# Start-up and x loads of a fused short convolution and ELU layer: band read in place, x of super 1 queued behind w_in, batch zeros over loaded rows, idle matmuls in super 0

## The chip, the cores and the metric

The kernel runs on one core of a Trainium2 chip. The time is the device time of one execution in microseconds. Executions of one kernel mostly agree within 0.3% of their median. Every ratio below is taken on one chip and within one set of rounds. The granted clock is the share of its full speed at which TensorE was allowed to run, by the profiler's records; "half clock" is a share of 0.5.

## The reference

`x` is (8, 4096, 192). A causal depthwise convolution of 7 taps is applied along the sequence, with one softmax-normalised set of taps for each of 8 heads of 24 channels. Then comes a two-layer network with ELU, 192 to 2048 to 192, over all 32768 tokens.

```python
w = softmax(weight)                       # (8 heads, 7 taps)
x_pad = concatenate([zeros(B, 6, D), x])  # zeros before each batch
out[b, s] = sum_k w[head, k] * x_pad[b, s + k]
h = out.reshape(32768, 192) @ w_in        # 192 -> 2048
g = where(h > 0, h, exp(min(h, 0)) - 1)
result = g @ w_out                        # 2048 -> 192
```

## The kernel before

The tokens are cut into 32 super-tiles ("supers") of 1024 tokens; four make a batch. Each super goes through 16 chunks of 128 hidden features. For each chunk TensorE makes H, ScalarE makes exp(H) into E, POOL clamps E to at most 1, and VectorE makes max(E - 1, H) as gT; one super later TensorE multiplies gT by w_out. H has three slots, so TensorE can be at most three chunks (or convs) ahead of VectorE. Two half convs per super are made by TensorE as well, with windows of x as weights and a band matrix `Tm` as the moving operand. Their result is evacuated to `csb`, written to HBM (`conv_slots`) and read back in another layout (`att`).

The band is built at the start: zeros are written to HBM, the 7 taps are written over the diagonal by a strided DMA, and all is read back as `Tk`, with the heads innermost. ScalarE and VectorE then each copy half of it to `Tm`, where the columns of one head lie together:

```python
# SyncE
sy.dma_start(diagonal, wprb[:].rearrange("p k h -> p (k h)")).then_inc(s_band, 16)
W(s_band, 32)
sy.dma_start(Tk[:], band[:, :, :]).then_inc(s_band, 16)
# ScalarE; VectorE does the other four heads in the same way
W(s_band, 48)
a.activation(Tm[:, HEADS // 2 :, :].rearrange("p h t -> p t h"),
             Tk[:, :, HEADS // 2 :], ACT.Copy).then_inc(s_tm)
# TensorE, in the conv
pe.matmul(H[...], xg[:, s % NXB, w, CPH * h : CPH * (h + 1)],
          Tm[:, h, PAD + c0 : PAD + c0 + nc_], ...)
```

POOL issues the loads of x and w_in, which convert from fp32 to bf16:

```python
X_AT = ((2, 0), (4, 1), (12, 2))       # (chunk, part of x of super s + 2)
# [cut]
def load_x(s, part):
    # [cut] part 0 exists only where a batch starts
    if part == 0:
        g.memset(xg[0:PAD, b, 0, :], 0.0).then_inc(s_z)
        g.dma_start(xg[PAD:P, b, 0, :], x_flat[t0 : t0 + P - PAD, :]).then_inc(s_x[b][0], 16)
        return
    # [cut] part 1: windows 0 (or 1) to 4; part 2: windows 5 to 8
for part in range(3):
    load_x(0, part)
W(s_band, 32)                          # the diagonal has landed
load_w_in(0)
W(s_w[0], 48)
g.dma_start(w_in[HP:P, :, c0:c1], w_in[0:HP, :, c0:c1]).then_inc(s_wdp, 16)
W(s_cv, 2)                             # both convs of super 0 are done
for part in range(3):
    load_x(1, part)
```

TensorE also runs 34 matmuls on zeros at the start and 24 after the first convs (`warm`), to keep its clock up.

Of the kernel before, what the change touches and what calls it, by code (L numbers as in the profile page):

```python
# [12 lines left out]
P = 128  # L13
# [3 lines left out]
HEADS = 8  # L17
# [4 lines left out]
CW = 122  # L22
# [6 lines left out]
NG3 = 2  # L29
LAG = -1  # L30
QA = 8
WARM = (34, 24)
HALF_STEPS = (10, 10, 6, 6, 10, 11, 11)

CONV_AT = ((4, 1, 1), (12, 2, 0))
EARLY_CONV = {1: (1, 0), 4: (1, 1), 12: (2, 0)}
XW = 5
X_AT = ((2, 0), (4, 1), (12, 2))
W_OUT_AT = 8

PIECES = (
# [6 lines left out]
def bass_lightweight_conv__then__act_elu_kernel(  # L48
# [84 lines left out]
    with ExitStack() as stack:  # L133
# [73 lines left out]
        NDMA_ATT = 6  # L207
        x_need, z_need, x_count, z_count = {}, {}, [0] * NXB, 0
        for s in range(NS):
            x_count[s % NXB] += 16 + 16 * (s % SPB == 0)  # L210
            z_count += s % SPB == 0
            x_need[s, 0] = x_count[s % NXB]
            x_need[s, 1] = 16 * (s // NXB + 1)
            z_need[s] = z_count
# [30 lines left out]
        @block.gpsimd  # L245
        def _gpsimd(g: bass.BassGpSimd):
            W = Waits(g)

            def load_x(s, part):
                b, t0 = s % NXB, s * SUP  # L250
                first = s % SPB == 0
                if part == 0 and not first:
                    return
                if s >= NXB:
                    W(s_cv, 2 * (s - NXB) + 2)
                if part == 0:
                    g.memset(xg[0:PAD, b, 0, :], 0.0).then_inc(s_z)
                    g.dma_start(  # L258
                        xg[PAD:P, b, 0, :], x_flat[t0 : t0 + P - PAD, :]
                    ).then_inc(s_x[b][0], 16)  # L260
                    return
                if part == 1:
                    w0, w1, row = int(first), XW, t0 - PAD + CW * first
                else:
                    w0, w1, row = XW, NWIN, t0 + SUP - P - CW * (NWIN - 1 - XW)
                src = bass.AP(
                    tensor=x_flat.tensor,
                    offset=row * D,
                    ap=[[D, P], [CW * D, w1 - w0], [1, D]],
                )  # L270
                g.dma_start(xg[:, b, w0:w1, :], src).then_inc(s_x[b][part - 1], 16)  # L271

            def load_w_in(k):
                c0, c1 = WCOLS[k]
                for j in range(3):
                    g.dma_start(  # L276
                        w_in[0:HP, j, c0:c1],
                        bass.AP(
                            tensor=moe_w_in.tensor,
                            offset=8 * j * FF + c0,  # L280
                            ap=[[CPH * FF, HEADS], [FF, 8], [1, c1 - c0]],
                        ),
                    ).then_inc(s_w[k], 16)

            for part in range(3):
                load_x(0, part)
            W(s_band, 32)
            load_w_in(0)
            W(s_w[0], 48)
            c0, c1 = WCOLS[0]  # L290
            g.dma_start(w_in[HP:P, :, c0:c1], w_in[0:HP, :, c0:c1]).then_inc(s_wdp, 16)
            W(s_cv, 2)
            for part in range(3):
                load_x(1, part)
            W(s_att[0], 16 * NDMA_ATT)
            load_w_in(1)
            for n in range(NP):
                s, i = divmod(n, NQ)
                if n == W_OUT_AT:
                    g.dma_start(  # L300
                        w_out[:, :, :], moe_w_out.rearrange("(q p) d -> p q d", p=FC)
                    ).then_inc(s_w[2], 16)
                for at, part in X_AT:
                    if at == i and s + NXB < NS:
                        load_x(s + NXB, part)
                for u in range(2):
                    W(s_exp, 2 * n + u + 1)
                    g.tensor_scalar(  # L308
                        out=E[:, n % NE, u, :],
                        in0=E[:, n % NE, u, :],  # L310
                        scalar1=1.0,
                        scalar2=0.0,
                        op0=ALU.min,
                        op1=ALU.max,
                    ).then_inc(s_clp)

        @block.scalar
        def _scalar(a):
            W = Waits(a)
            a.memzero(scr[:, 0:1]).then_inc(s_scr)  # L320
            W(s_scr, 1)
            a.activation(scr[:, 1:2], scr[:, 0:1], ACT.Exp)
            W(s_set, 2)
            a.activation(wex[:], wq2[:], ACT.Exp).then_inc(s_wex)
            W(s_band, 48)
            a.activation(  # L326
                Tm[:, HEADS // 2 :, :].rearrange("p h t -> p t h"),
                Tk[:, :, HEADS // 2 :],
                ACT.Copy,
            ).then_inc(s_tm)  # L330

            def evac(t, half):
                n_half = 2 * t + half
                W(s_mm2, n_half + 1)
                b = n_half % 2
                W(s_out[b], 32 * (n_half // 2))
                if (t, half) == last_half:
                    a.activation(  # L338
                        osb[:, b, 0, :, :].rearrange("p k d -> p (k d)"),
                        H[:, last_slot % 3, 0 : 2 * D],  # L340
                        ACT.Copy,
                    ).then_inc(s_oev)
                    W(s_od, 1)
                    out_group(a, t, half, 1)
                    return
                a.activation(  # L346
                    osb[:, b, :, :, :].rearrange("p g k d -> p g (k d)"),
                    ops[:, :, 0 : 2 * D],
                    ACT.Copy,
                ).then_inc(s_oev)  # L350

            for item in order:
                if item[0] == "c":
                    m = item[1]
                    if m == 1:
                        W(s_dw[0], 16)
                        read_att(a, W, 0, 0)
                        continue
                    W(s_cv, m + 1)
                    W(s_dw[m % 4], 16 * (m // 4))  # L360
                    a.activation(  # L361
                        csb[:, m % 4, :, :],
                        H[:, slot_of_conv[m] % 3, :].rearrange("p (b t) -> p b t", b=2),
                        ACT.Copy,
                    ).then_inc(s_ce)
                elif item[0] == "h":
                    n = item[1]
                    k = slot_of_pair[n] % 3
                    W(s_h, n + 1)
                    W(s_tt, 2 * (n - NE) + 2)  # L370
                    for u in range(2):
                        a.activation(  # L372
                            E[:, n % NE, u, :], H[:, k, GS * u : GS * (u + 1)], ACT.Exp
                        ).then_inc(s_exp)
                else:
                    _, t, half, r0, r1 = item
                    if r1 == NR:
                        evac(t, half)

        @block.vector  # L380
        def _vector(v):
# [21 lines left out]
                ALU.mult,  # L403
            ).then_inc(s_set)
            v.memset(H[:, 0:2, :], 0.0).then_inc(s_hz)
            W(s_band, 48)
            v.tensor_copy(  # L407
                Tm[:, 0 : HEADS // 2, :].rearrange("p h t -> p t h"), Tk[:, :, 0 : HEADS // 2]
            ).then_inc(s_tm)
            W(s_cv, 2)  # L410
            v.tensor_copy(
                csb[:, 1, :, :],
                H[:, slot_of_conv[1] % 3, :].rearrange("p (b t) -> p b t", b=2),
            ).then_inc(s_cd)
            for n in range(NP):
                s, q = divmod(n, NQ)
                if s >= NG3:
# [20 lines left out]
        def _tensor(pe):  # L438
# [17 lines left out]
            for item in order:  # L456
                if item[0] == "c":
                    m = item[1]
                    s, g = divmod(m, 2)
                    if m == 0:  # L460
                        W(s_tm, 2)
                        W(s_hz, 1)
                    for part in range(g + 1):
                        W(s_x[s % NXB][part], x_need[s, part])
                    W(s_z, z_need[s])
# [2 lines left out]
                    for hb in range(2):  # L468
                        for (w, c0, nc_, o) in PIECES[g]:
                            for q in range(4):  # L470
                                h = 4 * hb + q
                                ins = pe.matmul(  # L472
                                    H[SLOT * q : SLOT * q + CPH, k % 3,
                                      GS * hb + o : GS * hb + o + nc_],
                                    xg[:, s % NXB, w, CPH * h : CPH * (h + 1)],
                                    Tm[:, h, PAD + c0 : PAD + c0 + nc_],
                                    start=True,
                                    stop=True,
                                    tile_position=(0, SLOT * q),
                                )  # L480
                    ins.then_inc(s_cv)
                elif item[0] == "h":
                    n = item[1]
                    s, q = divmod(n, NQ)
                    if n == 0:
                        warm(WARM[1])
                    W(s_w[q // QA], 48)
                    W(s_wdp if q < QA else s_wd[1], 16)
                    W(s_att[s % 2], 16 * NDMA_ATT * (s // 2 + 1))
# [131 lines left out]
```

## Time and profile before

| | before |
|---|---|
| time, median (range, 3 runs) | 786.17 us (785.61 to 786.69) |
| profiled span | 783.9 us |
| first exp of chunk 0 | 29.62 us |
| from there to the first exp of super 1 | 26.69 us |
| a super after that | 22.95 us; 23.62 us for seven of them |

The last three rows come from the starts of ScalarE's exp instructions in the trace: chunk 0 of each super marks its beginning.

These are lines of the page of the kernel before: the span, TensorE's busy time, the granted clock in 40 slices (tenths), and the group of conv matmuls with their count, total busy us and mean ns.

```profile
span 783.9 us, 32275 instructions
...
PE 751.1 (96%) x13882; PEld 514.9 (66%) x13882; DVE 638.0 (81%) x1035; ACT 658.4 (84%) x1156; POOL 663.3 (85%) x1116
...
PEclk9889999999999999999999999999999999999999
...
L472 PE MATMUL H<-Tm,xg 128*24 128x122 bf16 (+1 forms) x2560 | 43.1, 213 | 7.4 <-DVE gT L421 5.0
```

TensorE is busy 96% of the span and about 98.5% of each 100 us window after the start.

The next lines are from the chain of waits of the kernel before, at the start: start in us, duration in us, what the chain stood on. "DMA" is a transfer from issue to landing.

```profile
5.50 3.22 DMA conv_band<-wprb
...
8.73 2.69 DMA Tk<-conv_band
...
11.44 2.55 ACT Tm L326
...
14.04 1.94 PE H L472 x75
...
17.25 6.92 DMA conv_slots<-csb
...
25.59 2.39 DMA att<-conv_slots
...
28.12 1.48 PE H L494 x6
```

Everything here is serial. Note the slot write at 17.25: 6.92 us, where the page's median for this transfer is 3.2 us. The packet records show what shares the DMA engines with it: 1152 packets of 384 bytes, x of super 1, between 19.3 and 24.5 us.

The third excerpt is the chain of the kernel before, inside super 6, one of the seven long ones.

```profile
175.06 0.19 POOL xg L257
175.25 0.54 POOL xg L258
...
175.82 2.34 POOL E L308 x4
178.16 0.75 POOL xg L271
...
178.94 0.64 POOL E L308
...
179.60 1.30 DVE gT L421 x2
```

POOL zeroes six rows (0.19 us of chain), issues the extra load of a batch start (0.54) and, a little later, the usual load (0.75). All of it stands between the clamps that VectorE and then TensorE wait for.

### The profile page before, as it was taken

Reading aid. Unit: us, or ns where it says so; the run is one execution under the profiler, and the core shown is the slowest. Engines: PE = TensorE matmul, PEld = TensorE weight load, DVE = VectorE, ACT = ScalarE, POOL = GpSimd, SP = SyncE. Lnnn points to the kernel's source line nnn. Section 1 sums busy time; section 2 is a strip of 40 time slices with the busy share of each in tenths; the row PEclk is TensorE's granted clock in tenths of the full one; section 3 lists DMA queues with packets and bytes.
Section 4 is the critical chain, followed back from the end, with each engine's and each line's share of the span. In section 5 each row is a group of like instructions: output and inputs, shape, how many; then the busy total and the mean of one; then the engine's idle time right before and its main releaser. Section 6 shows DMA issues by size and latency. Waiting matters only on the chain.

```text
span 783.9 us, 32275 instructions
## 1 busy us (share of the span) xinstructions
PE 751.1 (96%) x13882; PEld 514.9 (66%) x13882; DVE 638.0 (81%) x1035; ACT 658.4 (84%) x1156; POOL 663.3 (85%) x1116
## 2 busy tenths in 40 slices
PE   8479999999999999999999999999999999999997
PEld 3136666766666666666676666666667666666766
DVE  3378888888888888888888888888888888888893
ACT  2478888898889888888888888988888988898883
POOL 3488988988888898898898888889889889888882
PEclk9889999999999999999999999999999999999999
DMA  6674344344344435434444433443443444444212
GB/s 106 113 120 88 83 109 86 90 109 104 76 104 92 101 87 112 93 79 111 83 91 109 109 81 93 83 111 89 110 92 84 107 83 94 104 111 83 77 42 63
DMA packets 108031, 73.71 MB, mean 94 GB/s; under 512 B 45520, under 2 KB 106960, under 8 KB 107888
## 3 DMA queue, kind: packets, MB, share of 16 engines
q1 hardware_dynamic: 66344, 55.14, 22.2%
q0 software_dynamic: 41056, 16.11, 19.3%
q8 instruction: 109, 1.79, 0.9%
q10 hardware_dynamic: 488, 0.39, 0.2%
q14 instruction: 34, 0.28, 0.1%
HBM read 44.31 MB, written 42.24 MB: 110 GB/s over the span
## 4 chain that ended last, share of the span: by engine, by line
PE 41%; POOL 38%; DVE 11%; ACT 5%; DMA 2%; issue 2%; SPq 0%
POOL E L308 32%; PE H L494 24%; PE ops L523 16%; DVE gT L421 10%; POOL xg L271 6%; ACT E L372 5%; DMA conv_slots<-csb 1%; PE H L523 1%; POOL xg L258 0%; DMA conv_band<-wprb 0%; PE H L472 0%; DMA wq<-in_weight_dram 0%; DMA Tk<-conv_band 0%; ACT Tm L326 0%; DMA att<-conv_slots 0%
## 5 line engine op out<-in xcount | busy, mean ns | idle before, releaser
L421 DVE SCALAR_TENSOR_TENSOR gT<-E,H 128x512 f16<-128x512 f32 x1024 | 631.1, 682 | 123.1 <-POOL E L308 122.5
L308 POOL TENSOR_SCALAR E<-E 128x512 f32<-128x512 f32 x1024 | 602.0, 614 | 85.9 <-ACT E L372 77.4
L372 ACT ACTIVATE E<-H 128x512 f32<-128x512 f32 x1024 | 548.7, 597 | 97.8 <-PE H L494 81.4
L494 PE MATMUL H<-att,w_in 64*128 64x512 bf16 x3072 | 409.2, 379 | 19.6 <-DVE gT L421 10.1
L523 PE MATMUL ops<-w_out,gT 64*128 64x192 f16 x8064 | 414.7, 243 | 0.9 <-DVE gT L421 0.9
L523 PEld LDWEIGHTS ops<-w_out,gT 64*128 64x128 f16 x8064 | 342.7, 94 | 109.9 <-DVE gT L421 1.1
L494 PEld LDWEIGHTS H<-att,w_in 64*128 64x128 bf16 x3072 | 130.5, 94 | 125.0 <-DVE gT L421 30.8
L361 ACT ACTIVATE csb<-H 128x1024 bf16<-128x1024 f32 x63 | 64.5, 1023 | 5.4 <-PE H L472 5.2
L346 ACT ACTIVATE osb<-ops 128x768 f32<-128x768 f32 x63 | 51.5, 818 | 5.1 <-PE ops L523 5.1
L271 POOL DMA_DIRECT2D xg<-in_x_dram x64 | 53.1, 830 | 0.4 <-PE H L472 0.4
L472 PE MATMUL H<-Tm,xg 128*24 128x122 bf16 (+1 forms) x2560 | 43.1, 213 | 7.4 <-DVE gT L421 5.0
L472 PEld LDWEIGHTS H<-Tm,xg 128*24 128x24 bf16 x2560 | 33.5, 94 | 19.4 <-issue 16.5
L453 PE MATMUL ops<-zw 128*128 128x512 bf16 x58 | 16.5, 454 | 1.2 <-DVE zw L383 1.2
L276 POOL DMA_DIRECT2D w_in<-in_moe_w_in_dram x6 | 3.5, 584 | 15.7 <-DMA att<-conv_slots 10.3
L453 PEld LDWEIGHTS ops<-zw 128*128 128x128 bf16 x58 | 6.4, 113 | 10.6 <-issue 5.1
L326 ACT ACTIVATE Tm<-Tk 128x544 bf16<-128x544 bf16 x1 | 2.5, 2542 | 7.0 <-DMA Tk<-conv_band 7.0
L432 DVE COPY osb<-H 128x384 f32<-128x384 f32 x1 | 0.6, 558 | 8.9 <-PE H L523 8.9
L523 PE MATMUL H<-w_out,gT 64*128 64x192 f16 x128 | 5.6, 243 | 0.1
L523 PEld LDWEIGHTS H<-w_out,gT 64*128 64x128 f16 x128 | 5.2, 94 | 0.3 <-PE H L523 0.3
L258 POOL DMA_DIRECT2D xg<-in_x_dram x8 | 4.8, 602 | 0.3 <-issue 0.3
L407 DVE COPY Tm<-Tk 128x544 bf16<-128x544 bf16 x1 | 1.3, 1335 | 3.9 <-DMA Tk<-conv_band 3.9
L338 ACT ACTIVATE osb<-H 128x384 f32<-128x384 f32 x1 | 0.5, 490 | 4.7 <-PE H L523 4.7
(20 smaller groups left out, 11.3 us busy)
## 6 DMA issues: line engine op xcount, KB each, us to landing
out_dram<-osb SPq DMA_DIRECT2D x127, 192.0 KB, 2.4
conv_slots<-csb SPq DMA_DIRECT2D x64, 256.0 KB, 3.2
att<-conv_slots SPq DMA_DIRECT2D x189, 64.0 KB
xg<-in_x_dram POOLq DMA_DIRECT2D x40, 192.0 KB, 3.8
xg<-in_x_dram POOLq DMA_DIRECT2D x24, 240.0 KB, 4.5
w_in<-in_moe_w_in_dram POOLq DMA_DIRECT2D x6, 128.0 KB, 3.8
w_out<-in_moe_w_out_dram POOLq DMA_DIRECT2D x1, 768.0 KB, 8.8
w_in<-w_in POOLq DMA_DIRECT2D x1, 384.0 KB, 4.6
```

The lines of the kernel that those rows point to most:

```text
L258: g.dma_start(xg[PAD:P, b, 0, :], x_flat[t0 : t0 + P - PAD, :]).then_inc(s_x[b][0], 16)
L271: g.dma_start(xg[:, b, w0:w1, :], src).then_inc(s_x[b][part - 1], 16)
L276: g.dma_start(w_in[0:HP, j, c0:c1], bass.AP(tensor=moe_w_in.tensor, offset=8 * j * FF + c0, ap=[[CPH * FF, HEADS], [FF, 8], [1, c1 - c0]], ...
L308: g.tensor_scalar(out=E[:, n % NE, u, :], in0=E[:, n % NE, u, :], scalar1=1.0, scalar2=0.0, op0=ALU.min, op1=ALU.max,).then_inc(s_clp)
L346: a.activation(osb[:, b, :, :, :].rearrange("p g k d -> p g (k d)"), ops[:, :, 0 : 2 * D], ACT.Copy,).then_inc(s_oev)
L361: a.activation(csb[:, m % 4, :, :], H[:, slot_of_conv[m] % 3, :].rearrange("p (b t) -> p b t", b=2), ACT.Copy,).then_inc(s_ce)
L372: a.activation(E[:, n % NE, u, :], H[:, k, GS * u : GS * (u + 1)], ACT.Exp).then_inc(s_exp)
L421: v.scalar_tensor_tensor(out=gT[:, s % NG3, q, u, :], in0=E[:, n % NE, u, :], scalar=1.0, in1=H[:, slot_of_pair[n] % 3, GS * u : GS * (u + ...
L453: pe.matmul(ops[:, 0, :], zw[:, 0:P], zw[:], start=True, stop=True)
L472: ins = pe.matmul(H[SLOT * q : SLOT * q + CPH, k % 3, GS * hb + o : GS * hb + o + nc_], xg[:, s % NXB, w, CPH * h : CPH * (h + 1)], Tm[:, ...
L494: ins = pe.matmul(H[:, k % 3, GS * r : GS * (r + 1)], w_in[HP * r : HP * (r + 1), j, FC * q : FC * (q + 1)], att[HP * r : HP * (r + 1), s ...
L523: ins = pe.matmul(acc[:, g, D * kb : D * (kb + 1)], gT[HP * rt : HP * (rt + 1), t % NG3, q, g, t0 : t0 + P], w_out[HP * rt : HP * (rt + 1) ...
```

## The change

There are four parts. (1) The first conv reads `Tk` in place, so no copy stands before it; one copy on VectorE follows the csb copy. (2) POOL queues w_in at once, without waiting for the diagonal, and x of super 1 right behind it. (3) At a batch start the rows of window 0 are loaded with the others and then overwritten with zeros, which saves a DMA issue. (4) Two matmuls on zeros precede most H chunks of super 0, to keep the clock up.

```diff
-WARM = (34, 24)
+WARM = (34, 24, 2)
-X_AT = ((2, 0), (4, 1), (12, 2))
+X_AT = ((4, 1), (10, 0), (12, 2))
# POOL, load_x
-                if part == 0:
-                    g.memset(xg[0:PAD, b, 0, :], 0.0).then_inc(s_z)
-                    g.dma_start(
-                        xg[PAD:P, b, 0, :], x_flat[t0 : t0 + P - PAD, :]
-                    ).then_inc(s_x[b][0], 16)
+                if part == 0:
+                    if s:
+                        W(s_x[b][0], x_need[s, 0])
+                    g.memset(xg[0:PAD, b, 0, :], 0.0).then_inc(s_z)
+                    if s == 0:
+                        g.dma_start(
+                            xg[PAD:P, b, 0, :], x_flat[0 : P - PAD, :]
+                        ).then_inc(s_x[b][0], 16)
# POOL, start
-            W(s_band, 32)
             load_w_in(0)
+            for part in range(3):
+                load_x(1, part)
             W(s_w[0], 48)
             # [cut] the copy of w_in to the other partitions
-            W(s_cv, 2)
-            for part in range(3):
-                load_x(1, part)
# ScalarE and VectorE: the two half copies before the first conv go; VectorE, after its csb copy:
+            v.tensor_copy(Tm[:, :, :].rearrange("p h t -> p t h"), Tk[:]).then_inc(s_tm)
# TensorE, conv
-                                    Tm[:, h, PAD + c0 : PAD + c0 + nc_],
+                                    Tm[:, h, PAD + c0 : PAD + c0 + nc_]
+                                    if s
+                                    else Tk[:, PAD + c0 : PAD + c0 + nc_, h],
# TensorE, H
+                    elif n < NQ - 1:
+                        warm(WARM[2])
# [cut] semaphore counts
```

More of the change, by code (lines that the diff above doesn't have):

```diff
@@ L209, in bass_lightweight_conv__then__act_elu_kernel @@
         for s in range(NS):
-            x_count[s % NXB] += 16 + 16 * (s % SPB == 0)
+            x_count[s % NXB] += 16 + 16 * (s == 0)
             z_count += s % SPB == 0
@@ L253, in load_x @@
                     return
+                if part == 0:
[6 more added lines that the diff above has]
+                        ).then_inc(s_x[b][0], 16)
+                    return
                 if s >= NXB:
                     W(s_cv, 2 * (s - NXB) + 2)
-                if part == 0:
-                    g.memset(xg[0:PAD, b, 0, :], 0.0).then_inc(s_z)
-                    g.dma_start(
-                        xg[PAD:P, b, 0, :], x_flat[t0 : t0 + P - PAD, :]
-                    ).then_inc(s_x[b][0], 16)
-                    return
                 if part == 1:
-                    w0, w1, row = int(first), XW, t0 - PAD + CW * first
+                    w0, w1, row = int(s == 0), XW, t0 - PAD + CW * (s == 0)
                 else:
@@ L324, in _scalar @@
             a.activation(wex[:], wq2[:], ACT.Exp).then_inc(s_wex)
-            W(s_band, 48)
-            a.activation(
-                Tm[:, HEADS // 2 :, :].rearrange("p h t -> p t h"),
-                Tk[:, :, HEADS // 2 :],
-                ACT.Copy,
-            ).then_inc(s_tm)
             def evac(t, half):
@@ L405, in _vector @@
             v.memset(H[:, 0:2, :], 0.0).then_inc(s_hz)
-            W(s_band, 48)
-            v.tensor_copy(
-                Tm[:, 0 : HEADS // 2, :].rearrange("p h t -> p t h"), Tk[:, :, 0 : HEADS // 2]
-            ).then_inc(s_tm)
             W(s_cv, 2)
@@ L460, in _tensor @@
                     if m == 0:
-                        W(s_tm, 2)
+                        W(s_band, 48)
                         W(s_hz, 1)
+                    if m == 2:
+                        W(s_tm, 1)
                     for part in range(g + 1):
```

## The prediction

> **What bounds the kernel now.** From 56 us on, TensorE is busy about 98.5% of every 100 us window (the table of windows) at full clock; a super-tile (16 chunks) takes 22.95 us, so nothing here makes that rate better. But every fourth one (those loading x for a new batch; 7 in all) takes 23.62 us: 0.67 us more, and TensorE idles 0.54 us before the conv there. Before that, the chain of waits is serial: weights, band (written 5.50, 3.2 us; read back 8.73, 2.7 us), copy to Tm 11.44 (ScalarE 2.54 us), conv 14.04, its slots written from 17.25 (6.92 us to landing, against a median of 3.2 us), att read, first H matmul only at 28.12. Super 0 then takes 26.7 us, with TensorE busy 19.6 of the 28 us from 28 to 56 and half clock for 24.2 to 31.0 and 48.1 to 54.9 (clock records).
>
> **The steps.**
>
> 1. *Band in place.* The 2.55 us Tm copy leaves the chain, its replacement on VectorE (an estimated 2.7 us, twice the 1.33 us half) runs after the csb copy, off it. Price: the moving operand steps 16 bytes. The Trainium skill ("SBUF — State Buffer", Door 1: The DMA port swizzle) says every access to a new 16-byte line pays; no trace here shows it yet. The conv took 1.94 us cold; I expect about the same, warm but strided.
>
> 2. *Queue.* w_in no longer waits for the band, so it shares the DMA engines with the band's read-back; "DMA: Bandwidth & Descriptors" (Queues, rings and completion order) says engines round-robin between queues by packet. Tk has 128 packets of 93 ns, w_in 192 of some 200 ns: I expect Tk about 1.2 us later (12.6). Net conv start: 12.6 instead of 14.04, 1.4 us gained.
> In exchange, x of super 1 (1152 packets of 50 ns, 19 to 25 us in the packet records) no longer collides with the slot writes; part of the w_in copy still does. The second write should land near 19.5 instead of 24.17, the first H matmul start at 23.3 instead of 28.1: 4.8 us gained with step 1.
>
> 3. *Idle matmuls.* 28 of them, about 0.22 us warm: 6 us of TensorE time, mostly into its 8.4 us of idle time. They remove the half clock at 48 to 55 us, where the 12 H matmuls at 51.80 took 2.74 us on the chain instead of some 1.5. The first H chunk may still be cold. Small delays when two chunks are ready together. Net 1 us.
>
> 4. *Batch zeros.* Seven DMA issues (0.59 us) and their memset (0.25 us) leave chunk 2, where VectorE work is waiting for POOL; the memset reappears in chunk 10, in a stretch where POOL is also continuous. I take back 0.15 of the 0.67 us: 7 x 0.52 = 3.6 us.
>
> **Prediction: 776.8 us** (786.2 - 4.8 - 1.0 - 3.6), 8 in 10 within 772.5 to 781. Faster by over 2%: 0.05; within 2%: 0.94; slower: 0.01.
>
> **What would show it.** Step 1: first conv starts before 13 us; 80 matmuls within 2.2 us. Step 2: second slot write lands in 3 to 5 us; first H matmul at 22 to 24.5. Step 3: no half-clock stretch after 31 us; super 0 near 25.7 us. Step 4: all periods within 0.2 us of 22.95; no 0.54 us idle before the conv.
>
> **What would make it wrong.** Strided reads slowing the conv 3-fold (1.5 us lost or more); w_in traffic delaying the band read by 3 us; the w_in copy, now queued behind 1152 x packets, becoming what H waits for; idle matmuls hit at half clock (0.43 us each) delaying chunk 1; the memset in chunk 10 costing all of its 0.25 us.

## The result and the profile after

The changed kernel took 780.68 us (780.54 to 780.74, 4 runs) against 785.89 us of the kernel before on the same chip: ratio 0.9932, 95% interval 0.9915 to 0.9949. That is inside the predicted range, but the gain is 5.2 us where 9.4 us were predicted.

From the exp starts of the two traces, the 5.15 us of the spans divide as follows:

| stage | before | after | measured | predicted |
|---|---|---|---|---|
| start of the first H matmul | 28.12 | 26.80 | -1.32 | -4.8 |
| from there to the first exp | 1.50 | 0.87 | -0.63 | "may still be cold" |
| super 0, first exp to first exp of super 1 | 26.69 | 26.47 | -0.22 | -1.0 |
| supers 1 to 30 | 692.05 | 689.07 | -2.98 | -3.6 |

Lines of the page of the changed kernel that answer to those of before; the conv matmuls now stand in two groups, packed (`Tm`) and in place (`Tk`).

```profile
span 778.7 us, 32323 instructions
...
PE 755.2 (97%) x13910; PEld 515.3 (66%) x13910; DVE 639.0 (82%) x1035; ACT 655.4 (84%) x1155; POOL 660.0 (85%) x1109
...
PEclk9999999999999999999999999999999999999999
...
L466 PE MATMUL H<-Tm,xg 128*24 128x122 bf16 (+1 forms) x2480 | 41.1, 210 | 0.6 <-DVE gT L413 0.6
...
L466 PE MATMUL H<-Tk,xg 128*24 128x122 bf16 (+1 forms) x80 | 3.9, 363 | 5.4 <-DMA Tk<-conv_band 5.4
```

The in-place matmuls take 363 ns on average, the packed ones 210. The clock row no longer has the two 8s of the second and third slices.

The chain of waits of the changed kernel, over the start and most of super 0:

```profile
5.50 6.26 DMA conv_band<-wprb
...
11.78 3.67 DMA Tk<-conv_band
...
15.50 3.89 PE H L466 x74
...
20.67 2.17 DMA conv_slots<-csb
...
24.25 2.41 DMA att<-conv_slots
...
26.80 0.83 PE H L492 x6
27.63 0.67 PE ops L445 x2
...
30.66 0.88 PE ops L445 x2
...
32.29 0.54 PE ops L445 x2
...
39.25 0.54 PE ops L445 x2
```

Read against the chain of before, the copy is gone (-2.55). But the diagonal takes 6.26 instead of 3.22 (+3.04), the read-back 3.67 instead of 2.69 (+0.98), and the conv 3.89 instead of 1.94 (+1.95). Only the slot write pays for it: 2.17 instead of 6.92 (-4.75). The sum is -1.33, which is the -1.32 of the table. The idle matmuls (`PE ops L445`) stand on the chain four times, 2.63 us together.

The chain of the changed kernel inside super 9, an ordinary super, shows half of a period:

```profile
240.24 3.52 POOL E L310 x6
243.76 0.82 POOL xg L275
...
244.62 0.63 POOL E L310
...
245.27 1.30 DVE gT L413 x2
...
246.62 1.47 PE H L492 x12
```

The six clamps and the issue of a load at chunk 4 are on the chain (0.82 us; the load at chunk 12 of the same super takes another 0.73); TensorE, "busy" 99% of the time, is waiting for them through VectorE.

### The profile page after: what moved, and what is told of

Read it like the earlier page. It is cut to its first block, busy times and chain, and to the rows that moved or that the text cites. A ratio compares the mean times of both kernels' runs of the same rounds, so it can differ in the third digit from the quotient of the medians.

```text
span 778.7 us, 32323 instructions
## 1 busy us (share of the span) xinstructions
PE 755.2 (97%) x13910; PEld 515.3 (66%) x13910; DVE 639.0 (82%) x1035; ACT 655.4 (84%) x1155; POOL 660.0 (85%) x1109
## 4 chain that ended last, share of the span: by engine, by line
PE 41%; POOL 38%; DVE 11%; ACT 5%; DMA 2%; issue 2%; SPq 0%
POOL E L310 32%; PE H L492 24%; PE ops L521 15%; DVE gT L413 10%; POOL xg L275 6%; ACT E L367 5%; DMA conv_band<-wprb 1%; PE H L521 1%; PE H L466 1%; DMA Tk<-conv_band 0%; DMA wq<-in_weight_dram 0%; PE ops L445 0%; DMA att<-conv_slots 0%; DMA conv_slots<-csb 0%; POOL xg L258 0%
## 5 line engine op out<-in xcount | busy, mean ns | idle before, releaser
L275 POOL DMA_DIRECT2D xg<-in_x_dram x64 | 53.8, 842 | 0.4 <-issue 0.4
L466 PE MATMUL H<-Tm,xg 128*24 128x122 bf16 (+1 forms) x2480 | 41.1, 210 | 0.6 <-DVE gT L413 0.6
L466 PEld LDWEIGHTS H<-Tm,xg 128*24 128x24 bf16 x2480 | 31.6, 93 | 11.6 <-issue 11.6
L445 PE MATMUL ops<-zw 128*128 128x512 bf16 x86 | 23.2, 407 | 1.2 <-DVE zw L378 1.2
L445 PEld LDWEIGHTS ops<-zw 128*128 128x128 bf16 x86 | 7.4, 102 | 14.0 <-issue 7.0
L466 PE MATMUL H<-Tk,xg 128*24 128x122 bf16 (+1 forms) x80 | 3.9, 363 | 5.4 <-DMA Tk<-conv_band 5.4
L466 PEld LDWEIGHTS H<-Tk,xg 128*24 128x24 bf16 x80 | 2.2, 115 | 7.1 <-DMA Tk<-conv_band 5.9
```

The lines of the kernel that those rows point to most:

```text
L275: g.dma_start(xg[:, b, w0:w1, :], src).then_inc(s_x[b][part - 1], 16)
L445: pe.matmul(ops[:, 0, :], zw[:, 0:P], zw[:], start=True, stop=True)
L466: ins = pe.matmul(H[SLOT * q : SLOT * q + CPH, k % 3, GS * hb + o : GS * hb + o + nc_], xg[:, s % NXB, w, CPH * h : CPH * (h + 1)], Tm[:, ...
```

## The experiments

Eleven kernels were built from the changed one, and one (batch zeros alone) from the kernel before. All gave correct results.

| run | median | before, same chip | ratio (95%) |
|---|---|---|---|
| changed kernel | 780.68 | 785.89 | 0.9932 (0.9915 to 0.9949) |
| diagonal first | 780.24 | 786.89 | 0.9927 (0.9914 to 0.9940) |
| no idle matmuls | 781.99 | 786.89 | 0.9936 (0.9922 to 0.9951) |
| Tm copies back | 781.98 | 786.89 | 0.9948 (0.9933 to 0.9963) |
| all convs in place | 851.78 | 786.89 | 1.0833 (1.0817 to 1.0850) |
| batch zeros alone | 783.89 | 785.22 | 0.9974 (0.9959 to 0.9990) |
| x after the band | 782.25 | 785.22 | 0.9955 (0.9938 to 0.9973) |
| packed band | 779.63 | 785.22 | 0.9922 (0.9906 to 0.9939) |
| POOL loads at 6, 14 | 791.13 | 785.22 | 1.0066 (1.0051 to 1.0081) |
| POOL loads at 5, 13 | 769.48 | 785.96 | 0.9789 (0.9769 to 0.9808) |
| other start-up order | 780.03 | 785.96 | 0.9920 (0.9904 to 0.9937) |
| both of these | 770.25 | 785.96 | 0.9794 (0.9775 to 0.9814) |
| 5, 13 and x first | 768.77 | 786.16 | 0.9781 (0.9768 to 0.9795) |

My theory after the comparison was this: the early w_in and x traffic delays the small diagonal write (A), the 16-byte step slows the conv (B), and the idle matmuls cost on the chain what the clock gives back (C). The rivals were a slow write or a slow conv for other reasons (clock, DMA traffic), and idle matmuls that are pure gain or pure cost.

### Diagonal first

```diff
+            W(s_band, 32)
             load_w_in(0)
             for part in range(3):
                 load_x(1, part)
```

> The changed kernel with one wait put back: w_in (and x of super 1 behind it) is queued only after the band's diagonal has landed. Theory A (the early w_in and x traffic delays the small band write): the write takes about 3.2 us again instead of 6.3, the first conv starts at 11.8 to 12.8 us instead of 15.5; the slot writes then meet the later x and w_in traffic, so the second takes 3 to 5 us instead of 2.2. First H matmul near 25, total about 779 us. Rival (the write was slow for a reason of its own, not the queue): conv start stays near 15.5 and the total rises above 781.

The chain of waits of this run, four of its lines:

```profile
5.52 3.26 DMA conv_band<-wprb
...
8.79 2.65 DMA Tk<-conv_band
...
11.49 3.86 PE H L467 x80
...
16.62 4.90 DMA conv_slots<-csb
```

The write is back at 3.26 us and the read-back at 2.65, so theory A holds: the wait that the change removed had kept this small write short. The conv starts 4.0 us earlier, but the slot write then meets x and w_in (4.90 us), and the first H starts at 25.57 on a half clock (1.46 us instead of 0.83). Of the 4.0 us, 0.6 is left at the first exp (27.08 against 27.67), which the totals hardly resolve.

### x after the band

```diff
             load_w_in(0)
+            W(s_band, 48)
             for part in range(3):
                 load_x(1, part)
```

> The changed kernel, w_in as early as there, but x of super 1 queued only after the band has been read back. Theory A (w_in's packets are what the small band write stands behind): the write still takes 5 to 6.3 us and the first conv starts at 14 to 15.5 us. Theory B (x of super 1 is): the write is back at 3.2 us, conv starts near 12. In both, x now meets the slot writes again and the second takes 4 to 6 us: total 780 to 783.

Two lines of the chain of this run:

```profile
5.50 5.43 DMA conv_band<-wprb
...
10.96 2.59 DMA Tk<-conv_band
```

The diagonal took 5.43 us and the first conv began at 13.59 us, a little before the expected 14: w_in alone delays the write by 2.2 us, x on top by another 0.8. The read-back is as short as in the kernel before (2.69), so the 3.67 us of the changed kernel come from x of super 1 and what is queued behind it, not from w_in, whose last packet started at 11.0 us there, before the read-back was issued. The slot write grew to 4.04 us. The packet records show the same: the first 112-byte packet of the diagonal appears at 6.8 us in the kernel before and at 6.4 us in the run with the diagonal first, but at 8.9 us here and 8.4 us in the changed kernel; the write was issued at 5.5 us in all of them.

### Tm copies back

```diff
+ ScalarE and VectorE each copy half of Tk to Tm before the first conv, as before
- v.tensor_copy(Tm[:, :, :].rearrange("p h t -> p t h"), Tk[:]).then_inc(s_tm)
- else Tk[:, PAD + c0 : PAD + c0 + nc_, h]
```

> The changed kernel with the two Tm copies put back before the first conv, which then reads packed Tm. If the strided read is what made the first conv 3.9 us: conv starts 2.5 us later but takes 1.3 to 2.0 us, so the slot writes start 0 to 0.6 us later and the total is within 0.7 us of 780.7 (reading in place gained next to nothing). Rival (conv slow from clock or DMA traffic): conv still takes over 3 us and the total is 782.5 or more.

The conv took 1.94 us, at half clock. From the landing of the read-back to the end of the conv this run needs 4.53 us (2.55 + 0.04 + 1.94), the changed kernel 3.93: reading in place gains 0.6 us, not 2.55. The total is about 1 us longer than the changed kernel by ratio (0.9948 against 0.9932), a little more than expected, but the two intervals overlap; in the profiled run the read-back itself took 5.38 us instead of 3.67, with the same traffic queued. I have no explanation for that difference but the spread of start-up transfers between runs.

### All convs in place

```diff
-                                    Tm[:, h, PAD + c0 : PAD + c0 + nc_]
-                                    if s
-                                    else Tk[:, PAD + c0 : PAD + c0 + nc_, h],
+                                    Tk[:, PAD + c0 : PAD + c0 + nc_, h],
```

> The changed kernel with every conv reading the band in place, at a 16-byte step, to measure the stride alone at full clock. If the step costs four times the time per column (0.217 against 0.053 us per group of four 122-column matmuls), each half conv takes about 1.8 us instead of 0.65 and the total rises by 2 x 1.2 x 31 = 74 us where TensorE is the limit: 830 to 860 us. If the stride is nearly free at full clock, under 785 us.

The total was 851.78 us, within the expectation, and a super takes 25.35 us. Half a conv (40 matmuls) takes 1.94 us on the chain of this run, and 0.60 packed on the chain of the run with POOL loads at 5 and 13 below, both at full clock:

```profile
111.61 1.94 PE H L466 x40
...
263.40 0.60 PE H L467 x35
```

The starts of the matmuls tell it best: in the middle of this run, groups of four 122-column matmuls follow each other every 0.217 us; packed, in the changed kernel, every 0.053 us. In the first conv of the changed kernel the step is about 0.22 us at half clock and at full clock alike, so it is not TensorE's clock that sets this pace but the reading of the stepped columns. This settles theory B. Only the one step of 16 bytes was tried.

### Packed band

```diff
-    band = nc.dram_tensor("conv_band", (P, TW, HEADS), BF16).ap()
+    band = nc.dram_tensor("conv_band", (P, HEADS, TW), BF16).ap()
-                ap=[[HEADS * (TW + 1), P], [1, KSIZE * HEADS]],
+                ap=[[HEADS * TW + 1, P], [TW, HEADS], [1, KSIZE]],
-            sy.dma_start(Tk[:], band[:, :, :]).then_inc(s_band, 16)
+            sy.dma_start(Tm[:], band[:, :, :]).then_inc(s_band, 16)
# [cut] no Tk, no copy; wprb laid out by head
```

> The changed kernel with the band kept head by head in HBM, so that the read-back gives the packed Tm at once: no copy and no 16-byte step. Price: the diagonal is written in 1024 pieces of 14 bytes instead of 128 of 112. If stride alone slows the conv, it takes 1.3 to 2.0 us instead of 3.9; if the write grows by under 1.5 us, the first H matmul comes 0.5 to 2 us earlier than 26.8, total 779 to 780.5. If the 14-byte pieces take 3 us or more extra, the total is 781 to 783.

The diagonal in 1024 pieces of 14 bytes took 7.50 us instead of 6.26, within the w_in traffic; the conv took 1.94 us, at half clock. The first H started at 26.25 us. The total, 0.9922, is not distinguishable from the changed kernel's 0.9932.

### No idle matmuls

```diff
-WARM = (34, 24, 2)
+WARM = (34, 24, 0)
```

> The changed kernel without the idle matmuls between chunks of super 0 (the two warm-ups stay). Theory A (they cost on the chain about what the full clock gives back): super 0, first to 17th chunk, stays within 0.6 us of 26.5, total 780.0 to 781.3. Rival (they are what makes super 0 not slower): half-clock stretches return and the total is 1.5 us longer or more. A third possibility: they are pure cost, total 779 or less.

Super 0 took 26.59 us instead of 26.47, and the ratio is the same within its interval: theory C, no net gain from this part. (The median of 781.99 us lies above the expected range, but the kernel before was slower in these rounds too, 786.89 us against 785.89.) The half clock does return, as the table of windows of this run shows (start and end, length, TensorE busy, granted clock, DMA share, GB/s):

```profile
core 0: us, PE busy (x), PEclk, DMA share, GB/s
33.11:36.52 3.41, 1.48 (x46) 1.00 0.77 166
36.52:39.93 3.41, 2.74 (x14) 0.50 0.83 103
39.93:43.35 3.42, 2.24 (x18) 1.00 0.42 134
43.35:46.76 3.41, 1.45 (x14) 1.00 1.07 111
46.76:50.17 3.41, 2.99 (x50) 0.50 1.34 188
```

The windows are cut where the clock records change or would change, every 3.41 us. Each window in which TensorE was busy 1.45 or 1.48 us is followed by one at half clock. In the kernel before, the window from 44.69 to 48.11 (1.52 us busy, no idle stretch over 1.53 us) is followed by half clock, while those with 1.83 and 2.08 us busy, also at full clock, are not. The border is not sharp: in two other runs a full-clock window was followed by full clock with only 1.45 us busy (x after the band, 21.73 to 25.14) and 1.44 us (5, 13 and x first, 20.92 to 24.33).

### Batch zeros alone

This is the kernel before with only part 3 of the change.

```diff
-X_AT = ((2, 0), (4, 1), (12, 2))
+X_AT = ((4, 1), (10, 0), (12, 2))
# [cut] load_x and the counts as in the change
```

> The kernel before with the batch zeros alone changed. Theory: this part is separate from the start-up and gives the 3.0 us that the periods of the changed kernel show: the seven long super-tiles go from 23.62 to about 23.15 us (the memset in chunk 10 keeps 0.2 us), the start stays as before (first H matmul near 28.1 us), ratio about 0.996. Rival (the gain needs the other parts, or is given back elsewhere): ratio over 0.998.

Supers 1 to 30 took 689.04 us, as in the changed kernel (689.07), so this part is separate and worth 3.0 us in the periods. The total shows 2.0 us (0.9974), between the two expectations. In the profiled run the start happened to be slower although nothing in it was changed: the diagonal took 3.69 us, the slot write 8.47, and super 0 27.55 us with a half clock from 23.1 to 33.4 us. Five of the seven periods went from 23.62 to 23.12 us, two to 23.36. The two are supers 14 and 26, in the changed kernel and in every other run with these POOL places except all convs in place, whose periods are all 25.2 to 25.4 us; why, stays open.

### POOL loads at chunks 6 and 14

The chain of super 9 shows POOL's loads on it, and the timeline shows POOL waiting for ScalarE after them. So I tried to move the loads into that idle time, one super earlier, because x of super s + 1 has been used up after chunk 4 of super s.

```diff
-X_AT = ((4, 1), (10, 0), (12, 2))
+X_AT = ((6, 0, 2), (6, 1, 3), (14, 2, 3))   # (chunk, part, supers ahead)
+X_AT0 = ((4, 1, 2), (12, 2, 2))             # super 0 alone
```

> The changed kernel with POOL's x loads moved to chunks 6 and 14, one super-tile earlier, and the zeros to chunk 6: places where POOL waits for ScalarE in the trace, instead of chunks 4, 10 and 12 where it is on the chain. Theory (POOL's DMA issues and memset delay the chain there): super-tiles go from 22.95 to 22.75 to 22.85 us and the seven long ones equal the others, total 774 to 778. Rival (TensorE is the limit anyway, POOL's place does not matter): periods stay at 22.95 and the total within 1 us of 780.7.

This was slower, 791.13 us, with periods of 23.33 us (23.52 for the batch starts). The trace shows the mistake: the idle time was in front of the clamp of chunk 5 (1.06 us in this run), and the load at chunk 6 came behind that clamp, on the chain again, 0.84 us. The rival (places do not matter) falls too. Why this is slower than the changed kernel, where both loads are on the chain as well, is not shown.

### POOL loads at chunks 5 and 13

```diff
+X_AT = ((5, 1, 3), (13, 0, 3), (13, 2, 3))
+X_AT0 = ((4, 1, 2), (12, 2, 2))
```

> The changed kernel with POOL's x loads at chunks 5 and 13 and the zeros at chunk 13, one super-tile earlier. In the run with chunks 6 and 14, POOL stood idle 1.06 us before the clamp of chunk 5, and the load came just after it, on the chain (0.84 us). Theory (a POOL issue costs what it exceeds the idle time in front of that very clamp): the 0.9 us load now fits the idle time, periods 22.7 to 22.9 us, the batch ones within 0.1 us of the others, total 773 to 778. Rival (moving the loads one super-tile earlier is what made that run slow, by DMA traffic or waits): periods stay at 23.3 us, total near 790.

The total is 769.48 us, ratio 0.9789, more than expected. The periods are 22.65 us, batch starts and all others alike. The chain of one super of this run, by line:

```profile
by line: PE ops L522 47.8%; PE H L493 47.2%; PE H L467 5.2%
```

And three lines of POOL's timeline from the same super (start, us, what, idle before):

```profile
263.70 1.19 POOL L311 TENSOR_SCALAR E<-E 128x512 f32<-128x512 f32 x2 [0.28 <-ACT E L368]
264.84 0.89 POOL L276 DMA_DIRECT2D xg<-in_x_dram  x1
265.99 1.19 POOL L311 TENSOR_SCALAR E<-E 128x512 f32<-128x512 f32 x2 [0.26 <-ACT E L368]
```

The load at 264.84 now lies where POOL waited for ScalarE before, and 0.26 us of idle time is left behind it. The chain is TensorE alone: only now is TensorE the limit. The rival falls: these loads come one super earlier too, as in the slow run before. So it is the place that counts.

### Another start-up order, and all together

Three kernels tried to spare both the diagonal and the later transfers. All use the packed band. The first has w_in after the diagonal and x of super 1 after the second slot write:

```diff
+            W(s_band, 32)
             load_w_in(0)
             # [cut] the copy of w_in
+            W(s_dw[1], 16)
+            for part in range(3):
+                load_x(1, part)
```

> The changed kernel with a start-up in another order: band packed by head, w_in only after the diagonal has landed, x of super 1 only after the second slot write has landed. Theory (the band write waits behind w_in, the conv is slow by its stride, the slot writes collide with x): diagonal landed by 9 to 10.5 us, conv from 11.7 to 13.5 us on and 1.3 to 1.95 us long, slot writes 3 to 5 us beside the w_in copy, first H matmul at 22 to 24 us instead of 26.8; total 776.5 to 779. Rival (the early w_in is what the first H needs): H waits for the w_in copy, no gain.

Its chain, four lines:

```profile
5.32 3.99 DMA conv_band<-wprb
...
12.21 1.17 PE H L464 x73
...
14.65 2.62 DMA conv_slots<-csb
...
18.69 6.24 DMA att<-conv_slots
```

The diagonal, the conv (1.17 us: packed, at full clock) and the slot write are all as hoped. But the att read now shares the engines with x and takes 6.24 us instead of 2.41. The first H starts at 25.06 us, on a half clock, and the total is not distinguishable from the changed kernel's. It did not wait for the w_in copy; the wait moved to the next transfer. The second kernel adds the POOL places:

> The start-up order of the run before and the POOL places 5 and 13 together. If both gains are separate, they add: start earlier by 2.5 to 4.5 us and periods 22.7 to 22.9 us, total 768 to 775 us. If the POOL places do not help, it equals the start-up run.

The result is 770.25 us, ratio 0.9794: the periods are there, the start-up gain is not (first exp at 27.39 us, its att read took 6.20 us). The third puts x of super 1 directly behind x of super 0, before the diagonal, and w_in after it:

> The POOL places 5 and 13, the band packed by head, and x of super 1 queued at once behind x of super 0, with w_in only after the diagonal has landed: x's small packets are then over before the slot writes and the att reads. Theory (what matters is who shares the DMA engines with the chain's transfers): diagonal landed by 9.3 to 10.5 us, conv from 12 to 13.7 us, slot writes 2.5 to 4.5 us, att read 2.4 to 3 us instead of 6.2, first H matmul at 22 to 24 us; total 765.5 to 768.5. Rival (x's packets delay the band write as w_in's did): diagonal landed at 11 us or later and no gain on 769.5.

The att read is short again (3.11 us), but the diagonal took 6.63 us: x delays it as w_in did, so the rival holds for that transfer. The first H started at 25.20 us, 1.6 us before the changed kernel's; the total of 768.77 us (0.9781) is the best, though its interval overlaps that of the POOL places alone (0.9789). Only this one is clearly over 2% faster than the kernel before; the intervals of the POOL places alone and of the second kernel reach just past 0.98. By the quotient of the ratios (0.978 to 0.979 over 0.9932) this kernel and the POOL places alone beat the changed kernel by about 1.5%.

## Why the prediction was right or wrong

The range held the result and "within 2%" came true, with the gain about half of what was predicted. This owes something to luck: the result lies 0.3 us from the edge of the range, and gains that the prediction did not have (1.35 us more at the slot write, 0.63 at the first exp) made up for part of the 5 us that the diagonal and the conv lost. Term by term, in us:

| term of the prediction | predicted | measured |
|---|---|---|
| Tm copy off the chain | -2.55 | -2.55 |
| diagonal write | 0 (no term) | +3.04 |
| band read-back | +1.2 | +0.98 |
| first conv, in place | 0 | +1.95 |
| slot write, the rest of the 4.8 | -3.4 | -4.75 |
| first H to first exp | 0 | -0.63 |
| idle matmuls, super 0 | -1.0 | -0.22 |
| batch zeros | -3.6 | -2.98 |

- **Step 2 is the one that failed.** It let w_in compete "with the band's read-back" only and left out the write of the diagonal in front of it. The run with the diagonal first shows 3.26 us for that write and the changed kernel 6.26. The read-back came out near its predicted delay, but by luck: w_in was over by then, and it met x of super 1 (the run with x after the band). Its other half was right: the slot write no longer collides, and became shorter still than predicted.
- **Step 1 named the price and set it at zero.** "About the same, warm but strided" balanced a better clock against the step. The clock does not help a read that is limited by the step: 3.86 us at full clock (diagonal first) and 3.89 us at a partly half clock. "SBUF — State Buffer", Door 1: The DMA port swizzle, in the Trainium skill gave a mechanism, that each new 16-byte line costs, without a factor; this case measures four times the time of packed columns. That it is the lines which cost is not shown, since no run varied the step.
- **Step 3** had the direction of each part right: no half clock after 31.3 us, and some idle matmuls on the chain. Their sum was 0.8 us too good: 2.63 us of them were on the chain, and super 0 was only 0.12 us longer without them. The 0.63 us before the first exp come from the clock: the first H took 0.83 us at full clock instead of 1.48 at half. With the diagonal first, the same matmuls met half clock (1.46), so this gain depends on where the half-clock stretch happens to fall.
- **Step 4** was right in kind: the memset in chunk 10 is on the chain as well. What it takes back was sized at 0.15 us and measured 0.17 in five supers and 0.41 in two.
- **The reading of the bound** was too quick. The prediction took 98.5% busy time for TensorE's limit, "so nothing here makes that rate better". That was right for this change, but a super went from 22.95 to 22.65 us by moving two POOL loads. "Trainium Kernel Development and Optimization", Performance Expectations, in the Trainium skill warns that matmul busy time is a bad measure of how close a kernel is to its roofline; the chain of waits, with 38% of POOL on the page, had said so before.

## What to carry to other kernels

A wait before a large load may be there for a small transfer elsewhere that the chain depends on; before removing it, list every transfer in flight in that stretch, not just the next one. In these runs a DMA issue on POOL left the chain where the idle time directly in front of the next clamp held it (0.89 us into 1.06), and stood on the chain one chunk later (0.84 us), so place it by the timeline, not by the engine's idle total. And do not call an engine that looks 98% busy the limit before the chain of waits stays on it.

## What the Trainium skill lacked or had wrong

- "SBUF — State Buffer" (Door 1: The DMA port swizzle) says a new 16-byte line costs, and that one can stride "for free" up to 8 bf16 elements; it gives no factor, and it also asks for two accesses per line, which a step of 8 does not give. At a step of exactly 8 bf16 elements the moving operand ran at a quarter of the packed pace (0.217 against 0.053 us per group of 122 columns), the same at half and at full clock. The page on TensorE has nothing on strided moving operands.
- "DMA: Bandwidth & Descriptors" (Queues, rings and completion order) says each engine takes turns between queues by packet, and gives a packet as typically some 9 to 17 descriptors. It does not say whether a packet record of the trace is such a packet or one descriptor. The prediction took it for a packet, and turns of some 0.2 us do not give what was seen: the first packet record of the diagonal came 2.9 to 3.9 us after its issue instead of 0.9 to 1.4, and the landing at 5.4 to 7.5 us instead of 3.2 to 4.3, whenever other loads stood in POOL's queue behind x of super 0. If the records are descriptors, one packet of w_in takes an estimated 1.8 to 3.4 us (9 to 17 records of 0.2 us), which covers the 2.2 us that w_in alone added. These runs do not show where the turns fall.
- "TensorE: Matmul & The Clock Gate" (HAM oscillation — how this bites in real kernels) gives the rule that there be no idle gaps over about 3.4 us. The next heading of that page says that frequent short idles can halve the clock too, without a figure. Here the clock was halved with no TensorE idle stretch over 1.59 us: full-clock windows of 3.41 us with 1.45 to 1.52 us busy were followed by half clock, in the kernel before and the run without idle matmuls, and those with 1.83 us or more were not. Two windows of other runs, with 1.44 and 1.45 us busy, were not either, so this is no sharp threshold. The window length of the page agrees with the clock records.
- No page has the cost of very small writes to HBM in this form: 1024 pieces of 14 bytes landed in 3.99 us, 128 pieces of 112 bytes in 3.26 us, both with no w_in in front.
